# An attention loop that takes its steps two at a time, with a gap between building the routing's one-hot blocks and using them

## The chip, the cores and the metric

One core of one Trainium2 chip runs the kernel. The metric is device time in microseconds (us), lower is better; the kernel before takes 1090.47 us, the median of three runs (1088.94 to 1090.56).

## What is computed

Attention with queries averaged in pairs, then a mixture-of-experts layer that only some tokens enter, then a two-branch product through two more matrices:

```python
q_pool = q.reshape(B, H, S // 2, 2, D).mean(axis=3)          # B, H, S, D = 4, 8, 1152, 64
scores = np.matmul(q_pool, k.transpose(0, 1, 3, 2)) / sqrt(D)
attn = softmax(scores); x = np.matmul(attn, v)               # (4, 8, 576, 64) -> (2304, 512)
do_compute = x @ w_skip > 0; e_idx = argmax(x @ w_gate)       # 8 experts
x[t] += gate[t] * relu(x[t] @ w1[e]) @ w2[e]                  # where do_compute
out = ((x @ m1) * (x @ m2) @ w3) @ w_out                      # float32
```

## The kernel before

**The three parts.** The first part, about half of the time, is attention, and only it is touched. While it runs, spare slots of the engines convert weights that lie in memory as 64-bit numbers to float32 (the generator `conv_ops`, lines 111 to 119) and decide, for each finished batch of four, which token goes to which expert (the generator `route_ops`). Then follow the experts and the last product.

**A step of attention.** There are 16 pairs of heads (p) with nine blocks of up to 128 pooled queries each (l), so 144 steps i = 9p + l. One step's work has these pieces:

- S(i), `emit_s`, line 271: on TensorE the scores of 128 queries against 1152 keys, six matmuls of 384 columns (nine where l is 4, whose block holds 64 queries of each head), into three PSUM banks, the tile `s`.
- X(i), `emit_x`, line 282: VectorE takes the negated maximum over those 1152 columns.
- E(i), `emit_e`, line 294: ScalarE writes the exponentials to `p`, with their sum.
- T(i), `emit_t`, line 305: TensorE transposes `p` in nine blocks of 128x128, by a product with the identity, into the tile `s` of a later step.
- C(i), `emit_c`, line 324: three copies of 384 columns from there to `pt`, by ScalarE, VectorE, ScalarE.
- PV, `emit_pv`, line 341: attention times values. A unit is one of nine key blocks for both heads; the blocks l 0 to 4 of a pair of heads form one half (320 columns), l 5 to 8 the other (256 columns), so there are 18 units a pair of heads. Each of a unit's two matmuls fills 64 of the 128 columns of the array and shows as two instructions in the trace.

There are two tiles `s` of three banks, and two single banks `VB` that PV accumulates in, of which the routing borrows the one that is free.

**The order.** Nothing is scheduled by the compiler here: every engine runs its instructions in the order in which the loop writes them. Step i writes T(i-2) and C(i-2), then E(i-1), two units of PV, S(i) and X(i). T(i-2) and S(i) use the same tile, so S(i) must wait for the copies C(i-2) out of each bank. After the second group of T and C stands `side("D")`: one further piece of the routing if that is at a yield "D" (work for VectorE alone), else one further piece of the weight conversion. At the end of six of nine steps a piece of the routing at a yield "P" (products on TensorE, into a bank `VB`) follows.

**The routing.** Its tokens' slots come from one-hot blocks: `build(j)` compares a row of numbers with each token's slot on GpSimd (lines 441 and 444, four instructions a block; two blocks at first, in two buffers), and a product of two such blocks (line 465) adds them up. Three batches are routed inside the loop; the fourth comes after it.

Of the kernel before, what the change touches and what calls it, by code (L numbers as in the profile page):

```python
# [7 lines left out]
F32 = mybir.dt.float32  # L8
# [36 lines left out]
def body(ctx, tc, q, k, v, w9, w1, w2, m1, m2, w3t, wo, cst, mcst, ids, out, dbg=None):  # L45
# [89 lines left out]
    if True:  # L135
# [78 lines left out]
        def ld_kh(h):  # L214
            SP.dma_start(f(KH[0][64 * h:64 * h + 64]), f(KS[0][h][0:64]))
# [137 lines left out]
        def route_ops(b, hook=None, obs=None):  # L353
# [84 lines left out]
            def build(j):  # L438
                t = ob[j] = obs[j % len(obs)]
                for u in range(2):  # L440
                    E.tensor_scalar(t[:, 128 * u:128 * u + 128], iota[:, 0:128], hf_[:, 0, u, j:j + 1], None,
                                    op0=ALU.is_equal)
                for u, c0, n in ((0, 256, NSL), (1, 256 + NSL, NCNT)):
                    E.tensor_scalar(t[:, c0:c0 + n], iota[:, 0:n], hf_[:, 1, u, j:j + 1], idf[:, b, j:j + 1],
                                    op0=ALU.is_equal, op1=ALU.mult)

            parts = ((0, 0, NSL), (1, NSL, NCNT))
            for j in range(len(obs)):
                build(j)
            if len(obs) == NTT:  # L450
                yield "P"
                tp = tbank()
                for u, c0, n in parts:
                    for j in range(NTT):
                        t = ob[j]
                        PE.matmul(tp[:, c0:c0 + n], lhsT=t[:, 128 * u:128 * u + 128], rhs=t[:, 256 + c0:256 + c0 + n],
                                  start=(j == 0), stop=(j == NTT - 1))
                DVE.tensor_tensor(slots, tp[:, 0:NSL + NCNT], slots, op=ALU.add)
            else:
                for j in range(NTT):  # L460
                    yield "P"
# [102 lines left out]
        def wprime_fill():  # L564
            wp = tctx.enter_context(tc.tile_pool(name="wp", bufs=1, side="right", reuse_waits="tile"))
            CC = [wp.tile([128, 8, D], F32R, name=f"CC{x}") for x in "hl"]
            RW = [wp.tile([128, 8, 128], F32, name=f"RW{i}") for i in range(3)]
            WS = [[wp.tile([128, 8, 128], F32R, name=f"WS{x}{i}") for x in "hl"] for i in range(3)]
            wv.update(CC=CC, RW=RW, WS=WS)
            wov = wd["wo"].rearrange("(a p f) -> p a f", p=128, f=D)  # L570

            def ld_rw(u):
                SP.dma_start(RW[u % 3], wd["w3t"].rearrange("(u p a f) -> u p a f", u=8, p=128, f=128)[u])
            wv["ld"] = ld_rw
            for u in range(2):
                ld_rw(u)
                SP.dma_start(f(CC[1][:, 4 * u:4 * u + 4]), wov[:, 4 * u:4 * u + 4])
            ld_rw(2)
            yield
            for u in range(3):  # L580
                POOL.tensor_scalar(WS[u][0], RW[u], 1.0, 0.0, op0=ALU.mult, op1=ALU.add)
                POOL.tensor_tensor(WS[u][1], RW[u], f(WS[u][0]), op=ALU.subtract)
                ld_rw(u + 3)
                yield
            for a in range(8):
                POOL.tensor_scalar(CC[0][:, a], f(CC[1][:, a]), 1.0, 0.0, op0=ALU.mult, op1=ALU.add)
                POOL.tensor_tensor(CC[1][:, a], f(CC[1][:, a]), f(CC[0][:, a]), op=ALU.subtract)
                if a % 2:
                    yield
# [158 lines left out]
        with tc.manual_schedule():  # L748
# [20 lines left out]
            ld_kh(0)  # L769
            load_v(1)  # L770
            load(1)
            for i in range(NSTEP + 7):
                p, l = divmod(i, NT9)
                if i == NSTEP - NT9 + 1:
                    for _ in conv:
                        pass
                    ectx.close()
                    wfill = wprime_fill()
                if i > NSTEP - NT9:
                    next(wfill, None)  # L780
                if l == (4 if p == 0 else 1):
                    load(p + 2)
                if l == 7 and p >= 1:
                    load_v(p + 1)
# [7 lines left out]
                if (i - 36 - 8) >= 0 and (i - 36 - 8) % 36 == 0 and (i - 44) // 36 < NB - 1:  # L792
                    rts["g"] = route_ops((i - 44) // 36)
                    rts["k"] = next(rts["g"])
                if tr or ss:
                    st_s[i] = ps_s.tile([128, 3, 512], F32, tag="s", name="s")
                evac = []
                if tr:
                    for g in range(3):
                        emit_t(it, g, i, evac)  # L800
                        emit_c(it, g, EV[g], evac)
                        if g == 1 and i > 5:
                            side("D")
                if 1 <= i <= NSTEP:
                    emit_e(i - 1)
                for u in pvs:
                    if u:
                        emit_pv(*u)
                if ss:
# [3 lines left out]
                    if i == 0:  # L813
                        prep_q(1, DVE, 0, 256, sq[1])
                        for c in range(3):
                            prep_k(1, 384 * c, 384 * c + 384)
                        ld_kh(1)
                        for h in range(2):
                            prep_q(h, POOL, 256, SQ, sr[h])
                        next(conv)  # L820
                        DVE.tensor_copy(base, cs[:, C_EOFF:C_EOFF + NC_])
                        DVE.tensor_copy(csr, cs[:, C_U:C_U + 256])
                    if i == 2:
                        PE.matmul(VB[1][:, 0:128], lhsT=ones, rhs=tri, start=True, stop=True)
                        DVE.tensor_copy(iota[:, 0:128], VB[1][:, 0:128])
                        DVE.tensor_scalar(iota[:, 128:NSL], iota[:, 0:NSL - 128], 128.0, None, op0=ALU.add)
                        DVE.tensor_scalar(idf, idt, 1.0, None, op0=ALU.add)
# [3 lines left out]
                if ss and p == 0 and l < 3:  # L831
                    prep(1, l)
                if i == 4:
                    next(conv)
                if ss and l >= 6:
                    prep(p + 2, l - 6)
                if ss and l in ((3, 4) if p == 0 else (4, 5)):
                    prep(p + 1, l if p == 0 else l - 1)
            for _ in wfill:
                pass  # L840
            mctx.close()
# [204 lines left out]
```

## Time and profile before

| | |
|---|---|
| three runs | 1088.94, 1090.47, 1090.56 us |
| the profiled execution: its own time, its span | 1092.66 us, 1090.8 us |
| TensorE matmul / weight load busy | 1038.4 us / 839.9 us |
| VectorE, ScalarE, GpSimd busy | 598.0, 482.4, 387.0 us |
| mean granted TensorE clock | 0.984 of 2.4 GHz |
| attention's first transposes to its last PV product | about 15 to 558.5 us of the span |

The profiler records one execution. A busy matmul is not a matmul at its peak: matmuls overlap, so what a group of them costs is read from the start of the group to the start of the next one, in the timeline. The bracket at the end of a timeline row gives the idle time of that engine just before it, and what ended it. The granted clock is 1.00 at 2.4 GHz and 0.50 at 1.2 GHz.

### The profile page before, as it was taken

The numbers are of one execution on the slowest core, as the hardware profiler recorded it, in microseconds if no ns is written. First come the engines' busy times: TensorE is split into PE (matmuls) and PEld (weight loads), VectorE is DVE, ScalarE is ACT, GpSimd is POOL, SyncE is SP. The second block draws the span as 40 slices with busy tenths as digits, with TensorE's granted clock in tenths as the row PEclk, the third lists the DMA queues.
The fourth block names the chain that finished last, engine by engine and source line by source line (L and its number), as shares of the span: only waits on it lengthen the run. The fifth ranks groups of instructions, "written<-read, shape, count | busy, mean of one in ns | idle before, by whom it ended". The sixth has DMA issues, their size and how long they took to land. (4 is left out here: it accounts for less than half of the span.)

```text
span 1090.8 us, 16927 instructions
## 1 busy us (share of the span) xinstructions
PE 1038.4 (95%) x6101; PEld 839.9 (77%) x6101; DVE 598.0 (55%) x934; ACT 482.4 (44%) x902; POOL 387.0 (35%) x426
## 2 busy tenths in 40 slices
PE   6999999999999999999999999998799999999996
PEld 5677776677766777667667778786799998989895
DVE  5888887688986888755637422437531221212120
ACT  4666666565665666555532322334432221212121
POOL 4754433672536724351620523439201010101101
PEclk9999999999999999989998999999899999999999
DMA  9887778377973678714702761507101010101000
GB/s 256 259 239 192 216 218 232 101 182 212 268 224 98 185 214 256 183 40 101 238 20 74 247 225 40 190 25 243 34 11 50 10 49 20 39 20 39 29 2 30
DMA packets 68237, 144.83 MB, mean 133 GB/s; under 512 B 12960, under 2 KB 22560, under 8 KB 68130
## 3 DMA queue, kind: packets, MB, share of 16 engines
q1 hardware_dynamic: 63330, 129.28, 41.1%
q0 software_dynamic: 4800, 14.24, 4.0%
q8 instruction: 53, 0.87, 0.3%
q14 instruction: 54, 0.44, 0.1%
HBM read 86.21 MB, written 22.87 MB: 100 GB/s over the span
## 5 line engine op out<-in xcount | busy, mean ns | idle before, releaser
L282 DVE TENSOR_REDUCE sm<-s 128x1 f32<-128x1152 f32 x144 | 195.2, 1356 | 108.4 <-PE s L271 88.3
L324 ACT COPY pt<-s 128x384 f32<-128x384 f32 x288 | 138.0, 479 | 184.4 <-PE s L305 184.1
L271 PE MATMUL s<-k,q 128*128 128x384 f32 x864 | 204.3, 364 | 15.5 <-DVE k L197 7.8
L271 PEld LDWEIGHTS s<-k,q 128*128 128x128 f32 x864 | 147.2, 193 | 83.8 <-issue 41.7
L294 ACT ACTIVATE p<-s,sm 128x1152 f32<-128x1152 f32 x144 | 176.3, 1225 | 10.0 <-DVE sm L282 9.7
L341 PE MATMUL vb<-pt,vr 128*64 128x256 f32 (+1 forms) x1152 | 173.9, 422 | 4.5 <-DVE xr L490 2.1
L305 PE MATMUL s<-cs,p 128*128 128x128 f32 x1296 | 172.0, 279 | 2.9 <-ACT p L294 2.9
L305 PEld LDWEIGHTS s<-cs,p 128*128 128x128 f32 x1296 | 151.5, 144 | 12.1 <-ACT p L294 6.2
L956 DVE TENSOR_TENSOR ar<-b,ar 128x384 f32<-128x384 f32 x48 | 26.8, 558 | 191.9 <-PE b L952 191.9
L341 PEld LDWEIGHTS vb<-pt,vr 128*64 128x64 f32 x1152 | 70.7, 137 | 59.4 <-issue 23.7
L971 POOL DMA_INDIRECT out_dram<-ar,slots x18 | 18.1, 1003 | 272.1 <-ACT ar L970 267.4
L324 DVE COPY pt<-s 128x384 f32<-128x384 f32 x144 | 78.9, 548 | 5.1 <-PE s L305 5.0
L225 POOL TENSOR_TENSOR kl<-kr,kh 128x384 fp32r<-128x384 f32 x45 | 47.6, 1058 | 73.0 <-DMA k<-kl 70.2
L957 ACT CAST CVh<-ar 128x384 fp32r<-128x384 f32 x48 | 24.6, 513 | 108.8 <-DVE ar L956 108.8
L96 POOL TENSOR_TENSOR cm<-ch 128x512 f32<-128x512 f32 x40 | 43.0, 1079 | 66.6 <-DVE ca L119 46.1
L560 PE MATMUL b<-W1h,CVh 128*128 128x512 f32 x176 | 60.5, 403 | 1.2 <-ACT CVh L691 0.7
L560 PE MATMUL b<-W2h,CVh 128*128 128x512 f32 x176 | 60.7, 405 | 0.3
L560 PE MATMUL b<-WPh,CVh 128*128 128x512 f32 x144 | 57.3, 398 | 0.0
L560 PE MATMUL b<-WPh,CVl 128*128 128x512 f32 x144 | 56.9, 395 | 0.0
L560 PE MATMUL b<-WPl,CVh 128*128 128x512 f32 x144 | 56.8, 395 | 0.0
L970 ACT COPY ar<-b 128x512 f32<-128x512 f32 x18 | 10.6, 586 | 86.2 <-PE b L560 86.2
L224 POOL TENSOR_SCALAR kh<-kr 128x384 fp32r<-128x384 f32 x45 | 27.2, 604 | 57.2 <-PE s L271 53.6
(210 smaller groups left out, 1816.7 us busy)
## 6 DMA issues: line engine op xcount, KB each, us to landing
R<-in_w_dram SPq DMA_DIRECT2D x16, 1024.0 KB, 7.1
vr<-in_v_dram SPq DMA_DIRECT2D x16, 576.0 KB
kr<-in_k_dram SPq DMA_DIRECT2D x15, 576.0 KB, 6.2
qr<-in_q_dram SPq DMA_DIRECT2D x15, 576.0 KB, 6.6
k<-kh SPq DMA_DIRECT2D x30, 288.0 KB, 5.6
k<-kl SPq DMA_DIRECT2D x30, 288.0 KB, 6.4
q<-qnl SPq DMA_DIRECT2D x60, 144.0 KB, 3.4
ch<-in_w3t_dram SPq DMA_DIRECT2D x16, 512.0 KB, 5.6
```

The costliest lines, as they stand in the source:

```text
L96: POOL.tensor_tensor(m, hf, hf, op=ALU.mult)
L224: POOL.tensor_scalar(KH[i][:, cc], rawk[p][:, cc], 1.0, 0.0, op0=ALU.mult, op1=ALU.add)
L225: POOL.tensor_tensor(KL[:, cc], rawk[p][:, cc], f(KH[i][:, cc]), op=ALU.subtract)
L271: m = PE.matmul(sp[:, c, 0:384], lhsT=lt, rhs=kk[:, 384 * c:384 * c + 384], start=(n == 0), stop=(n == len(seq) - 1))
L282: DVE.tensor_reduce(sm, sp[:, :, 0:384], axis=AX.XY, op=ALU.max, negate=True)
L294: ACT.activation(pt, sp[:, :, 0:384], AF.Exp, bias=sm, scale=1.0, accum_out=SM[b][:, hp, c:c + 1])
L305: m = PE.transpose(tp[:, u * 128:u * 128 + 128], src[:, kt * 128:kt * 128 + 128], ident)
L324: m = (DVE.tensor_copy(o, i_) if eng is DVE else ACT.copy(o, i_)).ins
L341: PE.matmul(acc[64 * h:64 * h + 64, 0:n], lhsT=vr[:, h, kt, :], rhs=pt[:, kt, h, :], start=(kt == 0), stop=(kt == KT - 1))
L560: PE.matmul(o, lhsT=lh[a], rhs=rh[b_], start=(first and n == 0), stop=(last and n == len(order) - 1))
L956: DVE.tensor_tensor(cv, pb[:, 0:GT], av, op=ALU.mult)
L957: ACT.copy(CV[0][:, c], cv)
```

## The change

The loop runs over two steps a, a+1 at a time. For a pair it writes: E(a-2) and E(a-1); a routing piece at "P" if the table `BANK` names a bank for it; a side piece; the PV units that the table `PVU` names (three to five, mostly four); T and C of a-2 and then of a-1; a second side piece; a second routing piece at "P"; S(a), X(a), S(a+1), X(a+1). So T(a-1) now stands ahead of S(a), where T(i-2) and S(i) took turns before, and PV stands ahead of the transposes instead of behind them. Between building the first blocks and their products, the routing yields "C" twice, and each "C" uses up a side slot; at a "C" the slot still advances the weight conversion, and at a "D" it doesn't, as before. Loads and the preparation of q and k stay at their steps.

```diff
@@ route_ops
             for j in range(len(obs)):
                 build(j)
+            if not hook:
+                yield "C"
+                yield "C"
             if len(obs) == NTT:
@@ side
             if k and k in kinds:
                 rts["k"] = next(rts["g"], None)
-            elif k != "D":
+            if kinds != "P" and k != "D":
                 next(conv, None)
@@ the loop
-            for i in range(NSTEP + 7):
...
-                it = i - 2
-                tr = 0 <= it < NSTEP
-                ss = i < NSTEP
-                pvs = []
-                for n in (2 * i - 13, 2 * i - 12):
-                    pp, r = divmod(n, 18)
-                    pvs.append((pp, *divmod(r, 9)) if 0 <= pp < NP else None)
...
-                if tr:
-                    for g in range(3):
-                        emit_t(it, g, i, evac)
-                        emit_c(it, g, EV[g], evac)
-                        if g == 1 and i > 5:
-                            side("D")
-                if 1 <= i <= NSTEP:
-                    emit_e(i - 1)
-                for u in pvs:
-                    if u:
-                        emit_pv(*u)
-                if ss:
-                    for g in range(3):
-                        emit_s(i, g, evac)
-                    emit_x(i)
...
-                if l in (8, 0, 1, 3, 4, 5) and rts.get("k") == "P":
-                    free["b"] = VB[1] if l in (8, 0, 1) else VB[0]
-                    side("P")
+            PVU = {8: [(0, 0, k) for k in range(5)], 10: [(0, 0, k) for k in range(5, 9)],
+                   12: [(0, 1, k) for k in range(4)], 14: [(0, 1, k) for k in range(4, 8)],
+                   16: [(0, 1, 8)] + [(1, 0, k) for k in range(3)], 18: [(1, 0, k) for k in range(3, 7)],
+                   20: [(1, 0, 7), (1, 0, 8), (1, 1, 0), (1, 1, 1)], 22: [(1, 1, k) for k in range(2, 6)],
+                   24: [(1, 1, k) for k in range(6, 9)]}
+            BANK = {0: (1, 1), 2: (None, 0), 4: (0, 0), 6: (0, 0), 8: (1, 1), 10: (1, 1), 12: (0, 0), 14: (0, 0),
+                    16: (None, 1)}
+
+            def route_step(a, u):
+                n = BANK[a % 18][u]
+                if n is not None and rts.get("k") == "P":
+                    free["b"] = VB[n]
+                    side("P")
+
+            for a in range(0, NSTEP + 8, 2):
...
+                its = [i for i in (a - 2, a - 1) if 0 <= i < NSTEP]
+                for i in its:
+                    emit_e(i)
+                route_step(a, 0)
+                if a > 5:
+                    side("DC")
+                for pe in range(0, NP, 2):
+                    for dp, hf, kt in PVU.get(a - 9 * pe, ()):
+                        emit_pv(pe + dp, hf, kt)
...
+                for i in its:
+                    for g in range(3):
+                        emit_t(i, g, i + 2, evac[i + 2])
+                        emit_c(i, g, EV[g], evac[i + 2])
+                if a > 5:
+                    side("DC")
+                route_step(a, 1)
+                for i in (a, a + 1):
...
+                    if ss:
+                        for g in range(3):
+                            emit_s(i, g, evac[i])
+                        emit_x(i)
```

How the engines' queues stand. TensorE before, around the first product of one-hot blocks of a batch (L465): nine transposes (L305), two units of PV (L341, four matmuls), one step's scores (L271; two of the six stand here), the product, and round again.

```order
L305 MATMUL s<-cs,p 128x128 x9
L341 MATMUL vb_91<-pt_2201,vr 64x320 x4
L271 MATMUL s<-k_120,q_104 128x384
L271 MATMUL s<-k_120,q_105 128x384
...
L465 MATMUL vb_92<-ob_114 128x146
L465 MATMUL vb_92<-ob_114 128x18
L305 MATMUL s<-cs,p 128x128 x9
L341 MATMUL vb_91<-pt_2201,vr 64x320 x4
```

TensorE after, around the first such product of a batch (now L468): four units of PV, eighteen transposes, the product, both steps' scores (two of the twelve stand here), and the next product ahead of the next four units.

```order
L341 MATMUL vb_91<-pt_3230,vr 64x320 x4
L341 MATMUL vb_92<-pt_3430,vr 64x256 x4
L305 MATMUL s<-cs,p 128x128 x18
L468 MATMUL vb_91<-ob_114 128x146
L468 MATMUL vb_91<-ob_114 128x18
L271 MATMUL s<-k_120,q_104 128x384
L271 MATMUL s<-k_120,q_105 128x384
...
L468 MATMUL vb_91<-ob_115 128x146
L468 MATMUL vb_91<-ob_115 128x18
L341 MATMUL vb_92<-pt_3430,vr 64x256 x8
L305 MATMUL s<-cs,p 128x128 x18
```

A turn from one kind of matmul to the next comes three times for two steps, where it came six times.

VectorE before, from the last number that the blocks are built from (`hf`, L434): one maximum (L282), then the sum of the first product (L467), a copy (L324), two instructions of the conversion (L116, L119), and the next maximum.

```order
L434 CAST hf<-hl 128x20
L282 TENSOR_REDUCE sm<-s 128x1
L467 TENSOR_TENSOR slots<-vb_92,slots 128x164
L324 COPY pt_3591<-s 128x3x128
L116 SCALAR_TENSOR_TENSOR cm<-ch,cm 128x512
L119 SCALAR_TENSOR_TENSOR ca<-ch,cm 128x512
L282 TENSOR_REDUCE sm<-s 128x1
```

VectorE after, from the same cast on:

```order
L434 CAST hf<-hl 128x20
L282 TENSOR_REDUCE sm<-s 128x1 x2
L116 SCALAR_TENSOR_TENSOR cm<-ch,cm 128x512
L119 SCALAR_TENSOR_TENSOR ca<-ch,cm 128x512
L324 COPY pt_3596<-s 128x3x128 x2
L111 SCALAR_TENSOR_TENSOR cm<-cm,ch 128x512
L112 TENSOR_SCALAR cm<-cm 128x512
L470 TENSOR_TENSOR slots<-vb_91,slots 128x164
L282 TENSOR_REDUCE sm<-s 128x1 x2
```

The two maxima of a pair of steps stand next to each other, one side piece stands ahead of the two copies and one between them and the next two maxima, and the first product's sum comes a whole pair of steps after `hf`.

## Rows read from the trace of the kernel before

**Rows 1.** The page: busy us by engine (share of the span) xinstructions.

```profile
PE 1038.4 (95%) x6101; PEld 839.9 (77%) x6101; DVE 598.0 (55%) x934; ACT 482.4 (44%) x902; POOL 387.0 (35%) x426
```

**Rows 2.** Timeline, TensorE, one step: start us, us, engine, line, operation.

```profile
324.64 1.14 PE L305 MATMUL s<-cs,p 128*128 128x128 f32 x9
325.71 1.08 PE L341 MATMUL vb<-pt,vr 128*64 128x256 f32 x8
326.72 1.31 PE L271 MATMUL s<-k,q 128*128 128x384 f32 x6
327.87 1.14 PE L305 MATMUL s<-cs,p 128*128 128x128 f32 x9
```

**Rows 3.** Timeline, TensorE: nine transposes, and the last three of the same nine.

```profile
331.22 1.14 PE L305 MATMUL s<-cs,p 128*128 128x128 f32 x9
...
331.88 0.49 PE L305 MATMUL s<-cs,p 128*128 128x128 f32 x3
```

**Rows 4.** Timeline, TensorE, early steps without PV: scores straight behind transposes.

```profile
26.30 0.52 PE L271 MATMUL s<-k,q 128*128 128x384 f32 x2
...
26.84 1.14 PE L305 MATMUL s<-cs,p 128*128 128x128 f32 x9
27.89 0.62 PE L271 MATMUL s<-k,q 128*128 128x384 f32 x2
```

**Rows 5.** Timeline, all engines, the last steps of attention.

```profile
549.28 1.15 PE L305 MATMUL s<-cs,p 128*128 128x128 f32 x9
549.54 1.36 DVE L282 TENSOR_REDUCE sm<-s 128x1 f32<-128x1152 f32 x1 [1.64 <-ACT p L294]
550.93 1.22 ACT L294 ACTIVATE p<-s,sm 128x1152 f32<-128x1152 f32 x1
552.29 1.20 PE L305 MATMUL s<-cs,p 128*128 128x128 f32 x9 [0.64 <-ACT p L294]
553.21 0.56 DVE L324 COPY pt<-s 128x384 f32<-128x384 f32 x1 [1.85 <-PE s L305]
553.43 5.18 PE L341 MATMUL vb<-pt,vr 128*64 128x320 f32 x44
558.54 0.50 PE L560 MATMUL b<-CCh,WSh 128*128 128x512 f32 x1
```

**Rows 6.** Lines by form, TensorE, 553.40:558.54: of those 44, the ones of 256 columns.

```profile
L341 PE MATMUL vb<-pt,vr 128*64 128x256 f32 x36 | 4.1, 379 | 0.0
```

**Rows 7.** Timeline: one conversion piece beside GpSimd's work, the same alone.

```profile
287.41 1.04 POOL L96 TENSOR_TENSOR cm<-ch 128x512 f32<-128x512 f32 x1 [3.76 <-DMA ch<-in_m_dram]
287.91 1.09 DVE L111 SCALAR_TENSOR_TENSOR cm<-cm,ch 128x512 f32<-128x512 f32 x1
...
355.32 0.68 DVE L111 SCALAR_TENSOR_TENSOR cm<-cm,ch 128x512 f32<-128x512 f32 x1
356.04 0.43 DVE L112 TENSOR_SCALAR cm<-cm 128x512 int32<-128x512 int32 x1
```

**Rows 8.** Lines, VectorE, 20:560: xcount | busy us, mean ns | idle before.

```profile
L111 DVE SCALAR_TENSOR_TENSOR cm<-cm,ch 128x512 f32<-128x512 f32 x40 | 34.3, 856 | 1.1 <-POOL cm L96 1.1
L116 DVE SCALAR_TENSOR_TENSOR cm<-ch,cm 128x512 int32<-128x512 int32 x40 | 33.6, 839 | 0.0
L119 DVE SCALAR_TENSOR_TENSOR ca<-ch,cm 128x512 int32<-128x512 int32 x40 | 32.7, 817 | 0.7
L112 DVE TENSOR_SCALAR cm<-cm 128x512 int32<-128x512 int32 x40 | 24.7, 618 | 1.4
```

**Rows 9.** Waits, TensorE, 20:560: total us, times, longest us.

```profile
PE s L271 <- DVE pt L324: 7.0, 10, 1.2
PE vb L465 <- POOL ob L444: 5.9, 3, 2.0
```

**Rows 10.** Windows behind the first and third batch's first product: us, busy by engine, PEclk.

```profile
211.80:215.21 3.41, 3.41 (x16) 2.65 (x18) 1.50 (x3) 1.57 (x3) 3.41 (x6) 0.50 0.00 0
...
484.86:491.69 6.83, 6.73 (x25) 5.06 (x26) 1.48 (x3) 2.17 (x4) 5.81 (x10) 0.50 0.37 92
```

More of the change, by code (lines that the diff above doesn't have):

```diff
@@ L771, in body @@
             load(1)
-            for i in range(NSTEP + 7):
[L773 to L784, printed above, removed]
-                it = i - 2
-                tr = 0 <= it < NSTEP
-                ss = i < NSTEP
-                pvs = []
-                for n in (2 * i - 13, 2 * i - 12):
-                    pp, r = divmod(n, 18)
-                    pvs.append((pp, *divmod(r, 9)) if 0 <= pp < NP else None)
-                if (i - 36 - 8) >= 0 and (i - 36 - 8) % 36 == 0 and (i - 44) // 36 < NB - 1:
-                    rts["g"] = route_ops((i - 44) // 36)
-                    rts["k"] = next(rts["g"])
-                if tr or ss:
-                    st_s[i] = ps_s.tile([128, 3, 512], F32, tag="s", name="s")
-                evac = []
-                if tr:
-                    for g in range(3):
-                        emit_t(it, g, i, evac)
-                        emit_c(it, g, EV[g], evac)
-                        if g == 1 and i > 5:
-                            side("D")
-                if 1 <= i <= NSTEP:
-                    emit_e(i - 1)
-                for u in pvs:
-                    if u:
-                        emit_pv(*u)
-                if ss:
-                    for g in range(3):
-                        emit_s(i, g, evac)
-                    emit_x(i)
[L813 to L819, printed above, removed]
-                        next(conv)
[L821 to L827, printed above, removed]
-                if l in (8, 0, 1, 3, 4, 5) and rts.get("k") == "P":
-                    free["b"] = VB[1] if l in (8, 0, 1) else VB[0]
-                    side("P")
[L831 to L838, printed above, removed]
@@ new lines, in route_step @@
+            def route_step(a, u):
[4 more added lines that the diff above has]
+            for a in range(0, NSTEP + 8, 2):
+                if a >= 44 and (a - 44) % 36 == 0 and (a - 44) // 36 < NB - 1:
+                    rts["g"] = route_ops((a - 44) // 36)
+                    rts["k"] = next(rts["g"])
+                its = [i for i in (a - 2, a - 1) if 0 <= i < NSTEP]
[7 more added lines that the diff above has]
+                        emit_pv(pe + dp, hf, kt)
+                evac = {}
+                for i in (a, a + 1):
+                    if i < NSTEP or i - 2 in its:
+                        st_s[i] = ps_s.tile([128, 3, 512], F32, tag="s", name="s")
+                    evac[i] = []
+                for i in its:
+                    for g in range(3):
+                        emit_t(i, g, i + 2, evac[i + 2])
[3 more added lines that the diff above has]
+                route_step(a, 1)
+                for i in (a, a + 1):
+                    p, l = divmod(i, NT9)
+                    ss = i < NSTEP
+                    if i == NSTEP - NT9 + 1:
+                        for _ in conv:
+                            pass
+                        ectx.close()
+                        wfill = wprime_fill()
+                    if i > NSTEP - NT9:
+                        next(wfill, None)
+                    if l == (4 if p == 0 else 1):
+                        load(p + 2)
+                    if l == 7 and p >= 1:
+                        load_v(p + 1)
+                    if ss:
+                        for g in range(3):
+                            emit_s(i, g, evac[i])
+                        emit_x(i)
+                        if i == 0:
+                            prep_q(1, DVE, 0, 256, sq[1])
+                            for c in range(3):
+                                prep_k(1, 384 * c, 384 * c + 384)
+                            ld_kh(1)
+                            for h in range(2):
+                                prep_q(h, POOL, 256, SQ, sr[h])
+                            next(conv)
+                            DVE.tensor_copy(base, cs[:, C_EOFF:C_EOFF + NC_])
+                            DVE.tensor_copy(csr, cs[:, C_U:C_U + 256])
+                        if i == 2:
+                            PE.matmul(VB[1][:, 0:128], lhsT=ones, rhs=tri, start=True, stop=True)
+                            DVE.tensor_copy(iota[:, 0:128], VB[1][:, 0:128])
+                            DVE.tensor_scalar(iota[:, 128:NSL], iota[:, 0:NSL - 128], 128.0, None, op0=ALU.add)
+                            DVE.tensor_scalar(idf, idt, 1.0, None, op0=ALU.add)
+                    if ss and p == 0 and l < 3:
+                        prep(1, l)
+                    if i == 4:
+                        next(conv)
+                    if ss and l >= 6:
+                        prep(p + 2, l - 6)
+                    if ss and l in ((3, 4) if p == 0 else (4, 5)):
+                        prep(p + 1, l if p == 0 else l - 1)
```

## The prediction

> **What bounds the kernel now.** I read the busy times first, then TensorE's timeline in attention, then what it waits for. TensorE is busy 95% of the span, the next engine 55% [rows 1], so attention is a matter of TensorE's own sequence. One step without any wait [rows 2] shows it from group start to group start: transposes 1.07 us, four matmuls of PV (eight instructions) 1.01, scores 1.15, together 3.23. How much of that is the turn from one kind of matmul to the next?
>
> - Transposes run 0.66/6 = 0.11 us apart [rows 3], so nine take 0.99; the turn to PV adds 0.08.
> - At the end of attention 44 PV instructions, 36 of 256 columns and 8 of 320, take 558.54 - 553.43 = 5.11 us [rows 5, 6]. Counting two instructions side by side as one, and 320 columns as 1.25 times 256, that is 23 g + c = 5.11, and a step's group is 4 g + c = 1.01 [rows 2]; so g = 0.216 and c = 0.15. A unit of PV is 0.43 us (256) or 0.54 (320), and a group pays 0.15 at its edges.
> - The first two scores take 0.62 behind a turn, 0.52 in the middle of a group [rows 4]: 0.10.
> - Transposes straight behind scores pay nothing that shows.
>
> Turns therefore cost 0.08 + 0.15 + 0.10 = 0.33 us a step, 0.66 for two. Two steps take 6.46 us with PV at 256 columns, 6.90 at 320.
>
> The other thing to see is a chain that has slack today. From the end of a step's scores to its transposes, X, E and the hand-overs take 552.29 - 549.28 = 3.01 us [rows 5]; today a whole step of other TensorE work lies in that gap, with more to spare.
>
> **The change, part by part.**
>
> Turns. A pair of steps now has PV to transposes, transposes to scores, scores to PV, once each. Transposes to scores is in the trace, in early steps without PV: 27.89 - 26.84 = 1.05, so 0.06, and 0.10 in the first scores [rows 4], together 0.16. Scores to PV and PV to transposes are not there. Below, 0, if these edges are free; above, 0.33, what a whole PV group costs at both edges today. I take 0.23, PV's entry and its 0.15, since the shape that enters and leaves is the same. That makes 0.39 a pair against 0.66: TensorE's own time falls by 0.27 (0.17 to 0.50), over 72 pairs 19 us (12 to 36). A pair's own time becomes 18 x 0.11 + 2 x 1.05 + 0.39 + PV = 4.47 + PV: 6.20 with four units at 256, 6.63 with four at 320.
>
> The Trainium skill (TensorEngine Tiling (Array Packing), Key Properties) says that TensorE drains when the tiling mode changes, not just the tile. Transposes and scores both use the whole array, so by it their turn would be free and the sum some 11.5 us lower; the 0.16 us of the early steps speak against it.
>
> The chain. T(a-1) now stands ahead of S(a), and S(a+1) is the last thing ahead of the next pair. Round the loop: T(a-1) to S(a) 1.05, plus 0.07 because a group that waited starts slower (552.29 to 553.43 is 1.14 where 1.07 is usual) [rows 2, 4, 5]; S(a) 1.15; 0.26 until X(a) starts; X(a) 1.36; X(a+1) to the start of E(a+1) 1.39; E(a+1) to T(a+1) 1.36 [rows 2, 5]. Sum 6.63; the two maxima may overlap a little, so I take 6.6. A pair can't be shorter than that, however few turns it has. The nine pairs of 18 steps are by the table of units one of 5 x 320 (4.47 + 2.70 = 7.17), two of 4 x 320 (6.63 each) and six that the chain holds at 6.6: 60.0 us. The two steps of nine scores add 0.52 and about 0.3 (the second one partly hides): 60.8. Today 18 steps take 9 x 6.68 + 1.04 = 61.2. So of the 19 us on TensorE about 0.4 x 8 = 3 us come through.
>
> Conversion pieces. VectorE runs one piece between the pair's second copy and X(a). Counted from the start of T(a-1), that copy starts at 0.92 and takes 0.56 [rows 5], so the piece starts at 1.48; X(a) wants to start at 1.12 + 1.15 + 0.26 = 2.53. About 1.05 us are free. Five pieces convert two chunks: two of L111 and L112, one of L116 and L119, and L116 and L119 alone. At mean durations [rows 8] they take 1.5, 1.5, 1.7, 0.84, 0.82, late by 0.45, 0.45, 0.65, 0, 0, a mean of 0.31. L111 and L112 alone take 356.04 + 0.43 - 355.32 = 1.15 [rows 7], late by 0.10, which gives a mean near 0.1. I take 0.2, between the two. Of the 100 pieces 50 fall there, and in seven of nine pairs the chain is what counts: 50 x 0.2 x 7/9 = 8 us lost (4 to 12). The other piece of a pair runs while TensorE is at PV, ahead of copies whose banks are needed only after 18 transposes; I cost it at nothing, and if PV were shorter than it, it would delay S(a).
>
> The routing's first product. It waits for GpSimd's blocks, 5.9 us over three batches [rows 9], and behind it the granted clock is 0.50 (1.2 of 2.4 GHz), for 3.41, 3.41 and 6.83 us behind the three products [rows 10], of which the first and the last stand there. Half of those 13.7 us is lost, less what TensorE waited in them: 6. With two side slots between building and product, a pair of some 6.6 us later, the wait should go, and with it the fall of the clock: 12 us gained (0 to 13). Next in line is the product itself, which stays.
>
> Copies. TensorE waited 7.0 us in ten places for VectorE's copy out of the bank that scores want [rows 9]. Scores now come a pair's transposes later than the first copies: I take 4 gained (0 to 7), because where a route starts VectorE still has more ahead of the copies.
>
> Rest. Routing products behind T lengthen the chain, those ahead of PV lie in its slack; I let these cancel. GpSimd's and SP's queues get the same instructions at most a step earlier or later, which today's loads, made several steps ahead, cover; without that cover a load would cost its lateness once per pair of heads. First pairs and tail, where X and E lie bare: 1 us lost.
>
> Sum: -3 + 8 - 12 - 4 + 1 = -10 us. The profiled execution took 1092.66, with a span of 1090.8; the median of the runs is 2.2 below that execution, and against the median the forecast is 1080.5 us.
>
> **The rivals.**
>
> - The chain has more slack than I count, and TensorE's own sequence stays the bound: -19 - 12 - 7 + 1 gives 1053.5. For it: each hand-over in the chain is at its longest where nothing overlaps. Against: X, E and T take what they take in every row. Chance 0.12.
> - Slower: the conversion piece between the copies and X(a), stretched by GpSimd. L111 took 1.09 us beside a GpSimd instruction and 0.68 alone [rows 7]. If every instruction of a piece took 1.09, pairs would be late by 1.13, three in five times, a mean of 0.7: 50 x 0.7 x 7/9 = 27 us, and the time 1090.5 - 3 + 27 - 12 - 4 + 1 = 1099.5. It decides from a mean lateness of (3 + 12 + 4 - 1)/39 = 0.46 us, where everything else is used up. For it: the means alone give 0.31. Against: GpSimd is busy 35% of the span [rows 1], and the means already hold what it does to these instructions today. Chance 0.22. The Trainium skill (SBUF — State Buffer, Who interferes with whom) says that a VectorE instruction with two SBUF inputs contends with a GpSimd instruction that reads SBUF and that the later one waits for the first to end; by that rule L111, L116 and L119, all with two inputs, are at risk, and the 0.68 that became 1.09 agrees.
> - It gives nothing: the turns come back as waits for E, and the wait for blocks shows up at a later product: -3 + 8 - 4 + 1 = +2, but for half of the clock's 6: 1089.5. For it: the builder has two buffers, so later blocks depend on earlier products. Against: today there are three such waits, one a batch [rows 9]. Chance 0.12.
> - The turn from transposes to scores is free inside the pair: 72 x 0.16 = 11.5 less, 1069. Against it: both gaps of that turn in the early steps [rows 4]. Chance 0.04. It is what the rule on tiling modes, named above, would make of the turn.
>
> **How the numbers follow.** The forecast case has the remaining 0.50 and by its own bounds (8 as 4 to 12, 12 and 4 down to 6 and 2) runs from 1073 to 1091. About 0.2% (2.2 us) is what a measurement of this kernel can tell from no change. Faster: nearly all of the forecast case, the first and the last rival, 0.65. Within 0.2%: most of the third and the edge of the forecast, 0.12. Slower: the second rival, a little of the third and of the forecast's edge, 0.23. The range from 1064 to 1097 takes in the forecast, the third, most of the second up to a mean lateness of 0.63, and the fourth; it leaves out the first rival and the end of the second.
>
> **What would show it.** Right, in the profile of the changed kernel: 18 transposes in a row; a wait of up to 0.4 us for E ahead of T(a-1) in pairs at 256 columns and none at 320; transposes to scores 0.16; no wait for blocks at the first product, and no low clock behind it; X(a) starting late where two conversion instructions stand ahead. Wrong: pairs near 6.2 us (the chain doesn't bind), pairs over 7.1 (VectorE binds), or TensorE waiting for GpSimd or a load in a new place.

## The result, and the profile after

The changed kernel takes 1062.58 us (median of four runs, 1057.09 to 1064.62), the kernel before 1089.93 beside it: a ratio of 0.9739 [0.9706, 0.9772]. That is 27 us faster, where 10 were forecast, and 1.4 us below the lower end of the range. The profiled execution was the fastest of the four, 1057.09 us with a span of 1055.3.

The page, busy us by engine, answers to [rows 1]: TensorE lost 35 us of busy time, ScalarE 22, and VectorE and GpSimd stand as they did.

```profile
PE 1003.0 (95%) x6101; PEld 834.5 (79%) x6101; DVE 600.0 (57%) x934; ACT 460.7 (44%) x902; POOL 386.7 (37%) x426
```

TensorE's timeline in attention, answering to [rows 2]: start us, us, engine, line, operation, and in brackets its idle time before.

```profile
144.43 2.47 PE L305 MATMUL s<-cs,p 128*128 128x128 f32 x18
146.65 2.35 PE L271 MATMUL s<-k,q 128*128 128x384 f32 x12
148.94 1.95 PE L341 MATMUL vb<-pt,vr 128*64 128x256 f32 x16
150.82 2.47 PE L305 MATMUL s<-cs,p 128*128 128x128 f32 x18
153.04 0.60 PE L271 MATMUL s<-k,q 128*128 128x384 f32 x2
...
153.66 0.51 PE L271 MATMUL s<-k,q 128*128 128x384 f32 x2
...
157.74 2.46 PE L305 MATMUL s<-cs,p 128*128 128x128 f32 x18 [0.36 <-ACT p L294]
```

Two steps now take 150.82 - 144.43 = 6.39 us. The last row shows a wait of 0.36 us for the exponentials, ahead of the first nine of its transposes, T(a-2). The wait ahead of T(a-1) that was expected stands inside the eighteen and shows in the weight loads (0.30 us, in the rows of all engines further down). Attention's last PV group is followed by the first product of the next part at 525.76, where it was 558.54 [rows 5]:

```profile
525.76 0.50 PE L563 MATMUL b<-CCh,WSh 128*128 128x512 f32 x1
```

So attention became 32.8 us shorter. That repeats: in the profiled execution of a second round of the changed kernel this row starts at 526.01, and that execution took 1061.30. What lies behind attention takes 529.5 us in the first (1055.3 - 525.8), 533.5 in the second and 532.3 in the kernel before. That is the same work in all three, with 4 us between two executions of one kernel; the effect is in attention. (Leaving out the last 8 us of the span, the granted clock behind attention is 0.50 for 13.7 us in the first, 17.1 in the second and 17.1 in the kernel before; half of the 3.4 us between them is 1.7 of these 4 us.)

TensorE's waits between 20 and 560 us (total us, times, longest us) answer to [rows 9]. The wait for blocks is gone, and the wait for VectorE's copies is down from 7.0 to 0.2. In their place stands a wait for the exponentials, which was 0.6 us before. (L459 lies behind attention.)

```profile
PE s L305 <- ACT p L294: 13.7, 23, 1.8
PE vb L459 <- DVE R L444: 1.9, 4, 0.5
PE vb L490 <- DVE xr L493: 0.3, 1, 0.3
PE s L271 <- DVE pt L324: 0.2, 1, 0.2
```

The first batch's first product starts at 209.89 without a wait, and the stretch behind it (us; busy by engine; granted clock; DMA) answers to [rows 10]: the clock is 1.00 where it was 0.50. It stays at 1.00 from 23 us to the end of attention.

```profile
209.89 0.37 PE L468 MATMUL vb<-ob 128*128 128x146 f32 x2
```

```profile
209.90:213.30 3.40, 3.40 (x27) 3.16 (x26) 3.12 (x5) 1.27 (x4) 3.40 (x6) 1.00 0.41 106
```

### The profile page after: what moved, and what is told of

Same layout as the page of the kernel before. It is cut to its first block, busy times and chain, and to the rows that moved or that the text cites. A ratio compares the mean times of both kernels' runs of the same rounds, so it can differ in the third digit from the quotient of the medians.

```text
span 1055.3 us, 16801 instructions
## 1 busy us (share of the span) xinstructions
PE 1003.0 (95%) x6101; PEld 834.5 (79%) x6101; DVE 600.0 (57%) x934; ACT 460.7 (44%) x902; POOL 386.7 (37%) x426
## 5 line engine op out<-in xcount | busy, mean ns | idle before, releaser
L282 DVE TENSOR_REDUCE sm<-s 128x1 f32<-128x1152 f32 x144 | 189.1, 1349 | 20.2 <-PE s L271 17.6
L305 PEld LDWEIGHTS s<-cs,p 128*128 128x128 f32 x1296 | 140.3, 142 | 65.3 <-ACT p L294 57.7
L305 PE MATMUL s<-cs,p 128*128 128x128 f32 x1296 | 167.9, 279 | 21.7 <-ACT p L294 19.2
L271 PE MATMUL s<-k,q 128*128 128x384 f32 x864 | 178.6, 348 | 7.9 <-DVE k L197 7.7
L271 PEld LDWEIGHTS s<-k,q 128*128 128x128 f32 x864 | 149.9, 191 | 10.2 <-DVE k L197 8.2
L341 PE MATMUL vb<-pt,vr 128*64 128x256 f32 (+1 forms) x1152 | 155.1, 412 | 0.0
L324 ACT COPY pt<-s 128x384 f32<-128x384 f32 x288 | 122.5, 491 | 11.3 <-PE s L305 9.2
L341 PEld LDWEIGHTS vb<-pt,vr 128*64 128x64 f32 x1152 | 76.5, 136 | 59.3 <-issue 15.4
L324 DVE COPY pt<-s 128x384 f32<-128x384 f32 x144 | 79.2, 555 | 64.5 <-PE s L305 63.8
L224 POOL TENSOR_SCALAR kh<-kr 128x384 fp32r<-128x384 f32 x45 | 27.3, 606 | 46.3 <-PE s L271 45.3
```

What stands on the lines that cost most here:

```text
L224: POOL.tensor_scalar(KH[i][:, cc], rawk[p][:, cc], 1.0, 0.0, op0=ALU.mult, op1=ALU.add)
L271: m = PE.matmul(sp[:, c, 0:384], lhsT=lt, rhs=kk[:, 384 * c:384 * c + 384], start=(n == 0), stop=(n == len(seq) - 1))
L282: DVE.tensor_reduce(sm, sp[:, :, 0:384], axis=AX.XY, op=ALU.max, negate=True)
L305: m = PE.transpose(tp[:, u * 128:u * 128 + 128], src[:, kt * 128:kt * 128 + 128], ident)
L324: m = (DVE.tensor_copy(o, i_) if eng is DVE else ACT.copy(o, i_)).ins
L341: PE.matmul(acc[64 * h:64 * h + 64, 0:n], lhsT=vr[:, h, kt, :], rhs=pt[:, kt, h, :], start=(kt == 0), stop=(kt == KT - 1))
```

## The experiments

Two theories stood against each other. By the first, the chain from one pair's last exponentials to the next pair's (T, S, X, X, E) holds the changed kernel, so that most of what turns save is lost again. By the second, TensorE's own sequence holds it, and the saved turns come through. Besides, the gap and the pairing had to be told apart.

**The gap alone.** The kernel before, with the two yields "C" and the side slots that serve them:

```diff
+            if not hook:
+                yield "C"
+                yield "C"
...
-            elif k != "D":
+            if kinds != "P" and k != "D":
...
-                            side("D")
+                            side("DC")
```

> The loop of before, one step at a time, with nothing but the two turns between building the one-hot blocks and their products. Theory (the pairing brings more than was predicted, because the chain of maximum, maximum, exponential, transposes and scores is 6.37 us long in the trace after, not 6.6; the gap brings the predicted 12): 12 us less than before, 1078, ratio 0.989, no wait for blocks at the first product and no stretch at clock 0.50 behind it. Rival (the gap is what brought the 27 us, the pairing next to nothing): 1066 to 1070, ratio near 0.98. A third case, the gap brings nothing because a later wait takes its place: 1090.

Measured: 1078.23 us, ratio 0.9905 [0.9869, 0.9941], so 11 us gained, as the first theory had it. TensorE's waits between 20 and 560 us no longer hold one for blocks, and those for VectorE stand as before [rows 9]:

```profile
PE s L271 <- DVE pt L324: 6.9, 11, 1.2
PE vb L341 <- DVE xr L493: 2.1, 3, 0.7
PE vb L341 <- DVE lw L380: 1.9, 3, 0.6
```

From 18 us to the end of attention the clock is 1.00. The wait of 5.9 us and the low clock behind it (13.65 us at half speed, [rows 10]) went together, as the prediction had it.

**Pairing without the gap.** The changed kernel without these yields:

```diff
-            if not hook:
-                yield "C"
-                yield "C"
```

> The changed kernel without the two turns: products follow the building of their blocks at once. Theory: the wait for blocks (about 2 us) and the low clock behind it come back three times, 12 us more than the changed kernel, 1074 to 1075, ratio to before 0.986. Rival (the gap brought nearly all): 1085 to 1090. If the gap is worth nothing once steps are paired: 1062.

Measured: 1079.99 us, ratio 0.9918 [0.9889, 0.9947], 5 us above what was expected: the waits came back longer than the 2 us each that were counted. TensorE's timeline at the first batch's first product, and the stretch behind it by windows:

```profile
199.77 2.25 PE L305 MATMUL s<-cs,p 128*128 128x128 f32 x18
205.83 0.69 PE L465 MATMUL vb<-ob 128*128 128x146 f32 x2 [3.80 <-POOL ob L444]
206.46 3.88 PE L271 MATMUL s<-k,q 128*128 128x384 f32 x12
210.27 2.16 PE L341 MATMUL vb<-pt,vr 128*64 128x320 f32 x16
212.36 1.86 PE L305 MATMUL s<-cs,p 128*128 128x128 f32 x15
```

```profile
206.70:210.10 3.40, 3.40 (x12) 3.19 (x11) 1.54 (x2) 0.12 (x1) 3.40 (x7) 0.50 0.00 0
```

TensorE waits 3.80 us for a block, and behind it the clock is 0.50 for 3.40 us: twelve scores take 3.88 us where they take 2.35. This pair lasts 212.36 - 199.77 = 12.6 us. The same happens at the other two batches; the three waits make 11.4 us. The longest of the three is 3.8 us where it was 2.0 [rows 9]: the product now stands straight behind the second side slot, where PV and scores stood between.

How do the two parts add up? By the medians (1089.3 for the kernel before in that round) the gap alone gives 11.1 us and the pairing alone 9.3, both together 27.3. By the end of attention in the profiled executions it is 558.5, 543.4 (gap), 541.5 (pairing) and 525.8 (both), so -15.2 and -17.0 alone, -32.8 together: there they just add (the execution of the pairing alone was 3.6 us below its median). On top of the gap the pairing brings 1078.23 - 1062.58 = 15.7 us by the medians and 17.6 in attention. Each ratio is uncertain by 0.003 to 0.004, some 4 us, and whether there is more than a sum isn't settled.

**A shorter maximum in the changed kernel.** X takes the maximum over two of three banks only (the third is left out of it), which shortens the chain and VectorE's queue and leaves TensorE's instructions as they are:

```diff
-            DVE.tensor_reduce(sm, sp[:, :, 0:384], axis=AX.XY, op=ALU.max, negate=True)
+            DVE.tensor_reduce(sm, sp[:, 0:2, 0:384], axis=AX.XY, op=ALU.max, negate=True)
```

> The changed kernel with each maximum taken over two of the three banks, 768 of 1152 columns, so that the third bank is left out of the maximum. That shortens the chain by some 0.45 us for each of its two maxima and lets them start two matmuls earlier, 1.2 us a pair in all, and takes nothing from TensorE. Theory (the chain and what VectorE puts in it hold the pairs): the waits of the transposes for the exponential, some 20 us over 68 pairs in the trace after, nearly vanish, 1045 to 1050, ratio to before 0.96. Rival (TensorE's own sequence bounds the changed kernel): 1062, no change.

Measured: 1043.99 us, ratio 0.9596 [0.9561, 0.9632], 18.6 below the changed kernel and 1 below the expected range. The two maxima are shorter but don't start earlier, though that had been expected too: X(a) starts at the least 0.43 us behind the start of the last of its scores, in both kernels. So TensorE's own sequence alone is not what holds the changed kernel: the chain, with what VectorE puts in it, still costs it some 18 us. TensorE's timeline with the shorter chain, and its wait for the exponentials between 20 and 560 us (13.7 in the changed kernel):

```profile
302.92 2.19 PE L305 MATMUL s<-cs,p 128*128 128x128 f32 x18
304.86 2.33 PE L271 MATMUL s<-k,q 128*128 128x384 f32 x12
307.11 2.27 PE L341 MATMUL vb<-pt,vr 128*64 128x256 f32 x16
309.31 2.18 PE L305 MATMUL s<-cs,p 128*128 128x128 f32 x18
```

```profile
PE s L305 <- ACT p L294: 5.1, 8, 1.4
```

**The shorter maximum in the kernel before.** The same edit there is a control.

> The kernel before with each maximum taken over two of the three banks, so that the third bank is left out of the maximum: the control to the same edit of the changed kernel, which took 18.6 us off it. Theory (before, the chain has a whole step of slack and TensorE's own sequence is the bound): little, 1083 to 1089, ratio 0.994 to 1.0; what comes is VectorE's copies a little earlier, at most the 7 us that scores wait for them. Rival (VectorE's load bounds both kernels): 1070, as much as in the changed one.

Measured: 1076.85 us, ratio 0.9885 [0.9859, 0.9911]: a miss, 12 us gained where 0 to 7 were expected and the rival had 19. TensorE's waits between 20 and 560 us:

```profile
PE s L271 <- DVE pt L324: 5.1, 7, 1.2
PE vb L465 <- POOL ob L444: 4.7, 3, 1.6
```

The wait for copies fell from 7.0 to 5.1, that for blocks from 5.9 to 4.7, and the two for VectorE at L341 (2.1 and 1.9 in the kernel before) to 0.9 and 0.7. The clock is at 0.50 behind one of the three first products, for 3.4 us, and no longer behind all three. The shorter X thus relieves VectorE's queue and, it seems, through a slightly shorter wait the clock; it says nothing of the chain of before. A control with the gap in it is cleaner:

**The gap and the shorter maximum, no pairing.** Both edits above in the kernel before.

> The loop of before, one step at a time, with the gap and with the maximum over two of three banks (the third left out). Against the changed kernel with the same short maximum (1044.0 us, ratio 0.9596) this leaves the pairing alone as the difference, with the waits for the exponential and most of VectorE's load out of the way. Theory (half of the turns of TensorE is what the pairing saves, 0.33 us a pair of steps): 24 us more than 1044, 1066 to 1069, ratio 0.979 to 0.982. Rival (the pairing's gain is TensorE's waits for VectorE's copies, which the short maximum makes shorter too): 1050 to 1056.

Measured: 1068.06 us, ratio 0.98 [0.9771, 0.983], within what was expected. That is 10 us below the gap alone, so the shorter maximum gains something without any pairing: TensorE's three waits for VectorE fall from 6.9, 2.1 and 1.9 to 3.6, 0.9 and 0.7. In the changed kernel such waits came to only 0.5 in all, so they can't be its 18.6; there it is the wait for the exponentials that shrinks. From here to the paired kernel with the shorter maximum it is 1068.06 - 1043.99 = 24 us by the medians and 533.81 - 507.06 = 26.8 in attention: what pairing saves when the chain is short, some 5 us of waits for VectorE among it. Quiet groups alone give 72 x 0.41 = 29 (below).

**More turns, with the shorter maximum.** In 40 pairs the PV units are split, two ahead of the transposes and the rest between transposes and scores:

```diff
+                nu = 2 if its and a % 18 in (8, 12, 14, 18 % 18, 22 % 18) else len(units)
+                for u in units[:nu]:
+                    emit_pv(*u)
...
+                for u in units[nu:]:
+                    emit_pv(*u)
```

> The changed kernel with the short maximum (third bank left out), where TensorE is the bound, and in 40 of its pairs the PV units split: two units ahead of the transposes, the others between transposes and scores. No matmul more, but a turn from transposes to PV and one from PV to scores take the place of the one from transposes to scores. Theory (a PV group costs 0.33 us at its edges by the turns of the kernel before, and a turn can't be hidden): 0.25 to 0.33 us a pair, 10 to 13 us more than the short maximum alone, 1054 to 1057. Rival (turns hide in other waits, and the pairing's gain comes from elsewhere): 1044, no change.

Measured: 1077.42 us, ratio 0.9887 [0.9858, 0.9916], 33 above the kernel without the split, where 10 to 13 were expected. The run doesn't isolate a turn: PV between T(a-1) and S(a) also lengthens the chain, and TensorE's wait for the exponentials, between 20 and 560 us, went from 5.1 to 22.0 us.

```profile
PE s L305 <- ACT p L294: 22.0, 38, 1.8
```

These 17 us and the 13 that were expected for the turns (40 x 0.33, an estimate) make 30 of the 33. It shows what the order of the changed kernel is good for: PV stands where the chain has slack.

**The second side piece between VectorE's two copies.** In the changed kernel a conversion piece stands between the pair's second copy and X(a). Here it follows the first copy, and everything is still computed:

```diff
                     for g in range(3):
                         emit_t(i, g, i + 2, evac[i + 2])
                         emit_c(i, g, EV[g], evac[i + 2])
-                if a > 5:
+                    if i == a - 2 and a > 5:
+                        side("DC")
+                if a > 5 and not its:
                     side("DC")
```

> The changed kernel with the second side piece moved from behind VectorE's second copy, where it stands ahead of the maximum, to between the two copies. In the trace after the maxima start late by 0.29 us a pair in the mean, 20 us in all. Theory: most of that lateness goes and half to three quarters of it comes through, 1047 to 1053, ratio to before 0.963. Rival (the piece only moves the wait, scores then wait for the second copy): 1060 to 1065, with a new wait of the scores for VectorE's copy.

Measured: 1055.33 us, ratio 0.9688 [0.9652, 0.9725], 7.3 below the changed kernel by the medians, 5.6 by the ratios, and 6.8 by the end of attention (518.99 and 525.76): the best version of the study that leaves nothing out. It lies between the expected range and the rival's, and both things happen: the lateness goes, and scores wait for copies. The timeline shows the same piece, first in the changed kernel (VectorE, and one row of GpSimd; the last row is an L119 beside which GpSimd does nothing):

```profile
105.49 0.56 DVE L324 COPY pt<-s 128x384 f32<-128x384 f32 x1 [0.42 <-PE s L305]
...
105.96 1.04 DVE L116 SCALAR_TENSOR_TENSOR cm<-ch,cm 128x512 int32<-128x512 int32 x1
106.42 1.88 POOL L230 TENSOR_TENSOR qsum<-qr 128x576 f32<-128x576 f32 x1
107.04 1.80 DVE L119 SCALAR_TENSOR_TENSOR ca<-ch,cm 128x512 int32<-128x512 int32 x1
...
108.77 2.61 DVE L282 TENSOR_REDUCE sm<-s 128x1 f32<-128x1152 f32 x2
...
150.60 0.68 DVE L119 SCALAR_TENSOR_TENSOR ca<-ch,cm 128x512 int32<-128x512 int32 x1
```

And VectorE in this kernel:

```profile
103.19 0.56 DVE L324 COPY pt<-s 128x384 f32<-128x384 f32 x1 [0.27 <-PE s L305]
103.67 1.26 DVE L116 SCALAR_TENSOR_TENSOR cm<-ch,cm 128x512 int32<-128x512 int32 x1
104.96 0.88 DVE L119 SCALAR_TENSOR_TENSOR ca<-ch,cm 128x512 int32<-128x512 int32 x1
105.76 0.55 DVE L324 COPY pt<-s 128x384 f32<-128x384 f32 x1
106.23 2.61 DVE L282 TENSOR_REDUCE sm<-s 128x1 f32<-128x1152 f32 x2
```

From the start of the second copy to X(a) it is 108.77 - 105.49 = 3.28 us there and 106.23 - 105.76 = 0.47 here. What is late next is that copy, for which scores wait. TensorE's waits between 20 and 560 us here: 7.3 us for the exponentials in place of 13.7, 4.3 for copies in place of 0.2.

```profile
PE s L305 <- ACT p L294: 7.3, 11, 1.8
PE s L271 <- DVE pt L324: 4.3, 7, 1.1
```

**That version with the shorter maximum** asks whether anything but the chain is left.

> Both edits of the changed kernel: the second side piece between VectorE's copies, and the maximum over two of three banks (the third left out). Theory (both take away the same waits of the transposes for the exponential, and TensorE's sequence with its turns is the floor under them): 1039 to 1044, at most 5 us under the short maximum alone. Rival (two separate costs): the gains add up, 1035 to 1037.

Measured: 1042.88 us, ratio 0.958 [0.9557, 0.9603], the same as 1043.99. With a short chain the place of the piece no longer matters: the two gains are one and the same time.

**The changed kernel once more**, beside the last runs.

> The changed kernel as it is, on the same chip as the three beside it. 1060 to 1064 us, ratio to before 0.972 to 0.977.

Measured: 1061.24 us, ratio 0.9738 [0.971, 0.9767], as expected.

## Why the prediction missed

The direction and the gap were right; the pairing was priced wrongly. By the prediction's terms the pairing alone should have cost 2 us (-3 + 8 - 4 + 1), and in attention it gained 17. (Two sums of the prediction are off beside that. By the bounds it names, its forecast case runs from 1076.5 to 1092.5 and not from 1073 to 1091; and its fourth rival takes off 11.5 us whole, though by its own chain little of that would come through. Neither matters for the miss.) To see where the pairing gained, I add up for every group of attention on TensorE the time from its start to the start of the next group, in the timelines of four kernels, from about 12 us of the span to the first product behind attention:

| us | gap alone | changed | gap, short X | changed, short X |
|---|---|---|---|---|
| transposes (L305) | 162.0 | 158.1 | 159.3 | 150.2 |
| PV (L341) | 163.3 | 162.3 | 161.4 | 152.4 |
| scores (L271) | 187.8 | 173.8 | 183.4 | 173.1 |
| the rest, mostly the routing's products | 17.4 | 18.9 | 17.4 | 18.9 |
| sum | 530.5 | 513.1 | 521.5 | 494.6 |

**Turns** were the first mis-sized step: "TensorE's own time falls by 0.27 ... over 72 pairs 19 us". Groups without waits show what it is. I take the medians, from group start to group start, between 60 and 500 us in the two kernels with the short maximum:

| us | step by step, twice | in pairs | saved |
|---|---|---|---|
| transposes | 2 x 1.074 | 1.940 | 0.21 |
| PV, 256 columns | 2 x 1.014 | 1.879 | 0.15 |
| scores | 2 x 1.158 | 2.262 | 0.05 |
| sum | 6.49 | 6.08 | 0.41 |

That is 0.41 us saved a pair where 0.27 was counted, over 72 pairs 29 us. The last two columns of the first table say 27, and with their waits for VectorE and for the exponentials taken out, 28. The early steps with a group of nine, from which 0.06 was taken for the first gap, had overstated it: behind eighteen there is no gap, and the first two scores still take 0.60 where 0.51 is usual (153.04 and 153.66). The Trainium skill (TensorEngine Tiling (Array Packing), Key Properties) says that a change of the tiling mode, and not just of the tile, drains TensorE. That the gap is missing agrees with it; the 0.09 us at the first scores are a cost of the turn all the same.

**The chain** was the second: "A pair can't be shorter than that", 6.63 or 6.6 us. All engines in the changed kernel, from T(a-1) to T(a+1) (PEld is the weight load with which a transpose starts):

```profile
145.69 0.96 PEld L305 LDWEIGHTS s<-cs,p 128*128 128x128 f32 x9 [0.30 <-ACT p L294]
146.65 2.35 PE L271 MATMUL s<-k,q 128*128 128x384 f32 x12
148.06 2.62 DVE L282 TENSOR_REDUCE sm<-s 128x1 f32<-128x1152 f32 x2 [0.30 <-PE s L271]
149.46 1.22 ACT L294 ACTIVATE p<-s,sm 128x1152 f32<-128x1152 f32 x1 [1.92 <-DVE sm L282]
150.72 1.22 ACT L294 ACTIVATE p<-s,sm 128x1152 f32<-128x1152 f32 x1
152.08 0.42 PEld L305 LDWEIGHTS s<-cs,p 128*128 128x128 f32 x4 [0.30 <-ACT p L294]
```

The loop takes 152.08 - 145.69 = 6.39 us. T(a-1) to X(a) is 2.37, not 2.53, because T(a-1) takes 0.96 to the first scores: the 0.07 for a group that waited is not there, nor the turn's 0.06. The two maxima take 2.62 together, not 2.72, so X(a) to E(a+1) is 2.66 and not 2.75. E(a+1) to T(a+1) is 1.36, as counted. By the sum the chain and the late pieces were to give back 16 + 8 = 24 of the saved time. The table's second column less its fourth says 18.5, most of it in PV's groups (9.9, the time until the transposes may start) and in the transposes (7.9, the time between the two steps' transposes). The wait that is left with the short maximum adds 4 (5.1 against 0.9 with the gap and the short maximum), and the first pair (below) accounts for as much, so that 19 answer to the 24. This 19 is the least certain of the sizes here (see the stretch without the routing).

**The late pieces** were near the upper end of what was said. With the piece between the copies, the same sums fall by 12 us in transposes and PV (158.1 to 154.2 and 162.3 to 154.0), while scores take 5.6 more, waiting for copies; 8 (4 to 12) was the forecast. So of the 18.5 about 12 may be the lateness, which would leave 6 for the bare chain with the first pairs, where 16 were counted for the chain. The second rival, a piece stretched by GpSimd, does happen: L119 took 1.80 us at 107.04 where it takes 0.68 alone. By the Trainium skill (SBUF — State Buffer, Who interferes with whom), such an instruction waits for the GpSimd instruction that started first. The rows agree: L119 ends 0.54 us after GpSimd's 1.88 us, started at 106.42, were over. But VectorE's conversions by lines, over 20 to 525 us (xcount | busy us, mean ns), stay near [rows 8]; and X(a) starts later behind the last of its scores than usual by a mean of 0.29 us (20 us over 68 pairs), short of the 0.46 from which that rival decides:

```profile
L111 DVE SCALAR_TENSOR_TENSOR cm<-cm,ch 128x512 f32<-128x512 f32 x40 | 36.5, 913 | 0.0
L119 DVE SCALAR_TENSOR_TENSOR ca<-ch,cm 128x512 int32<-128x512 int32 x40 | 33.3, 833 | 0.7
L116 DVE SCALAR_TENSOR_TENSOR cm<-ch,cm 128x512 int32<-128x512 int32 x40 | 31.1, 777 | 0.0
L112 DVE TENSOR_SCALAR cm<-cm 128x512 int32<-128x512 int32 x40 | 23.7, 594 | 1.4
```

**Copies** were the third: 4 us of 7.0. Nearly all of it went, and with it two waits of PV for the routing's work on VectorE, 2.1 and 1.9, which the sum had left out: 10.9 us with the gap alone, 0.5 now.

**The routing's first product** was right: 12 forecast; without the pairing 11 by the medians and 15 in attention's profiled execution. With the pairing, where the waits without the gap are longer (11.4 us for 5.9), it is 17 by the medians (1079.99 - 1062.58) and 16 in attention. The third rival, that it gives nothing, falls with it.

**The rest** was put at 1 us. The first pair of steps, from its transposes to the next pair's, takes 11.62 us where it took 8.89 in the kernel before and 7.68 with the gap alone; so 4 us, and the routing's products 1.5 more.

**A stretch without the routing** shows the terms from another side. The nineteenth to the thirty-sixth step, from transposes to transposes, lie ahead of the routing's first products. An eighth of a term stands here for its share of these 18 steps.

| us | counted | measured |
|---|---|---|
| kernel before | 61.2, and 0.9 of waits for copies | 62.7 (80.42 to 143.12) |
| gap alone | the same | 62.8 |
| gap and short maximum | | 61.5, without a wait of TensorE's matmuls |
| changed | 60.8, 1.0 for late pieces, 0.4 of waits for copies | 61.3 (83.11 to 144.43) |
| changed, short maximum | | 59.2 |

So the old steps took 0.6 us more than was counted, and the new ones 0.9 less. The short maximum takes 62.8 - 61.5 = 1.3 off the old steps, 1.1 of it in the scores, which wait for copies; the copies' 4 make 0.5 here. Of the 61.5 the turns alone would save 9 x 0.41 = 3.7, where the prediction's 19 make 2.4. Only 0.2 of that comes through, so the chain and the late pieces take 3.5 back, where their 24 make 3.0. In this stretch, then, turns and copies were counted too low, by 1.3 and 0.8, and the chain with its late pieces was too low as well, by 0.5. In the next 90 steps, which hold the routing, the pairing saves more: 331.8 us with the gap alone and 318.1 changed, which is 2.7 for 18 steps where it is 1.5 here.

Added up over attention: turns 28 for 19, chain and late pieces 19 for 24, copies 10 for 4: 9 + 5 + 6 = 20 us better than forecast, the rest 4 worse. That makes 16 of the 19 by which the pairing was off (2 + 17); 3 us stay open. The forecast's mechanism, a saving on TensorE that the chain partly takes back, is what the short maximum shows. The steps that failed are the sizes of two of its terms, the turns (19 us counted, 28 measured) and the waits for VectorE's copies (4 of 7.0 counted, 10 gone); both show in the whole of attention and in the quiet stretch. As a bound for one pair the chain's 6.6 was too long, since 6.39 is measured; but whether the chain with its late pieces was counted too high in sum stays open: the whole of attention says so, the quiet stretch doesn't. Also open is why attention shows 32.8 us and the medians 27.3: the profiled execution of before was 2.7 above its median, that of after 5.5 below, the latter in the part behind attention.

## What to carry to other kernels

When a sequence on one engine is made shorter so that a chain through other engines becomes its bound, measure the loop of that chain where its parts overlap, not as a sum of single hand-overs at their longest: 0.2 us in a loop that runs 72 times would be 14 us, more than the whole forecast of 10. Hold the sum of quiet rows against a whole cycle of the kernel before: here 62.1 us were counted, waits included, where its trace has 62.7. List all waits that the new order removes, not only the longest row. Then look at what stands in the chain's queues without being part of it: moving one side piece on VectorE from behind the copies to between them gave 7 us more.

## What the runs showed of the hardware that was not expected

- Two maxima of 1152 columns, one behind the other on VectorE, took 2.62 us where one takes 1.35.
- A turn from transposes to scores costs no gap behind eighteen transposes, and 0.09 us in the first two scores.
- A VectorE instruction of 0.68 us took 1.80 us beside a GpSimd instruction of 1.88 us; [rows 7] showed 1.09.
- A wait is paid for a second time in the clock: in pairing without the gap, 3.80 us of waiting were followed by 3.40 us at 0.50, half of which is lost. In the kernel before with the shorter maximum the three waits came to 4.7 us in place of 5.9, and the clock fell once in place of three times.
